# One overlapping 5 KB run per partition for the four shifted k rows, with the front of the convolution done in place

## The chip, the cores and the metric

The kernel runs on one core of one Trainium2 chip. The metric is device time in microseconds (us), the median over executions; a figure called "span" is the length of one profiled execution, about 2 us shorter than its time. Inside an execution, times count from the start of the span.

## The reference, cut to what matters

```python
def _A_ref(q, k, v, shift_k, ssm_k, ssm_D):          # B, S, D = 1, 2048, 640; ks = 4
    k_pad = jnp.pad(k, ((0, 0), (ks - 1, 0), (0, 0)))
    k_shift = jnp.zeros_like(k)
    for t in range(ks):
        k_shift = k_shift + k_pad[:, t:t + S, :] * shift_k[:, ks - 1 - t][None, None, :]
    kv = k_shift * v
    # ... long convolution of kv with ssm_k by FFT, plus kv * ssm_D, gives y
    return q * y
x = A_q
h = x + _A_ref(_layernorm(x), A_k, A_v, A_shift_k, A_ssm_k, A_ssm_D)
h2 = h + _B_ref(_layernorm(h), B_w_gate, B_w_up, B_w_down)   # silu(x@gate) * (x@up) @ down
```

Each output row needs four neighbouring rows of k. The kernel cuts the 2,048 rows into four blocks of 512 and each block into two halves of 256 rows.

## The kernel before

For each half of a block, the "front" loads four shifted copies of k (k0 to k3, 0.33 MB each) and v, multiplies and adds them to kv, mirrors the first half through TensorE (kvr), and forms the sum and the difference xe and xo (the tile xeo). TensorE then transforms xeo to X. VectorE multiplies X with the transformed filter G and accumulates into A; TensorE transforms A back ("inverse"); after a layer norm the rows hl are transposed by DMA into hT, and the up and down products of the FFN follow.

```python
def conv_front(j, p_load, p_calc):
    kv = []
    for half in (0, 1):
        ...                                             # block 0 uses other tiles and queues
            ks = [front.tile([P, 2, D], BF16, name=f"k{jj}", bufs=2 if jj == 0 else 1) for jj in range(4)]
            v = front.tile([P, 2, D], BF16, name="v")
        for jj in range(4):
            load2(eng, ks[jj][:], kk, j, half, jj)      # four loads, each shifted by one row
        load2(eng, v[:], vv, j, half)
        for jj in range(4):
            nc.vector.tensor_mul(ks[jj][:], ks[jj][:], w4[:, jj:jj + 1, :].to_broadcast([P, 2, D]))
        ...                                             # three adds, times v -> ks[0] is kv
        if half == 0:
            kvr = front.tile([P, 2, D], BF16, name="kvr")
            mirror(ks[0], kvr)
    xeo = front.tile([P, 4, D], BF16, name="xeo")       # own tile for xe and xo
    nc.vector.tensor_add(xeo[:, 0:2, :], kv[1][:], kvr[:])
    nc.vector.tensor_sub(xeo[:, 2:4, :], kv[1][:], kvr[:])
    return xeo
...
prio(1500)                                              # the 2 MB of down weights
wd = big.tile([P, NF, D], BF16, name="wd")
nc.sync.dma_start(out=wd[:, 0:13, :], in_=...)       # and a small load of the rest
...
def inverse(A, x, xln):                                 # twice per block: two hl, two transposes
    ...
        nc.sync.dma_start_transpose(hT[:, :, q * P:(q + 1) * P], hl[:])
```

## Time and profile before

| kernel before | value |
|---|---|
| time, median of three (a fourth, taken later, makes it 316.98) | 316.9 us (316.35 to 317.23) |
| span of the profiled execution | 315.9 us |
| VectorE (DVE) busy in all | 237.6 us (75%) |
| TensorE (PE) busy in all | 277.0 us (88%) |

The first view is busy time by stretch, cut at three events: the first y of block 0 (VectorE at 60.19 us), 100 us, and the end of VectorE's last accumulation (246.64 us). Columns: the stretch, its length, then busy time with instruction count for PE, weight loads, DVE, ACT and POOL, then the granted TensorE clock and the DMA share.

```profile
core 0: us, PE busy (x) PEld busy (x) DVE busy (x) ACT busy (x) POOL busy (x), PEclk, DMA share, GB/s
0.00:60.19 60.19, 35.27 (x227) 22.90 (x228) 39.16 (x54) 29.46 (x51) 9.83 (x18) 1.00 0.79 231
60.19:100.00 39.81, 35.89 (x208) 21.16 (x207) 37.08 (x52) 33.34 (x67) 4.61 (x3) 0.91 0.55 157
100.00:246.64 146.64, 140.78 (x767) 72.70 (x765) 140.24 (x187) 83.23 (x172) 20.11 (x10) 1.00 0.52 138
246.64:315.90 69.26, 65.11 (x382) 35.91 (x382) 21.14 (x44) 22.46 (x46) 5.58 (x6) 0.99 0.30 81
```

Length minus DVE busy is VectorE's idle time: 2.73 us from 60 to 100, and 6.40 us in the 146.64 us after. In both stretches VectorE is nearly full; then 69 us of matmuls remain. So the kernel ends when the last accumulation ends, plus the tail.

The next view is VectorE's timeline near 90 us. `k_1375`, `k_1403`, `k_1373` and `k_1400` are tiles of block 2; xeo at 89.74 is block 1's.

```profile
start us, us, engine line op out<-in xcount [idle before <-releaser]
...
85.30 0.82 DVE L174 TENSOR_TENSOR k_1375<-k_1375,k_1376 128x1280 bf16<-128x1280 bf16 x1
...
89.00 0.82 DVE L172 TENSOR_TENSOR k_1403<-k_1403,w_92 128x1280 bf16<-128x1280 bf16 x1
89.74 0.82 DVE L182 TENSOR_TENSOR xeo<-k_765,kvr 128x1280 bf16<-128x1280 bf16 x1
...
95.36 0.82 DVE L172 TENSOR_TENSOR k_1373<-k_1373,w_92 128x1280 bf16<-128x1280 bf16 x1
96.09 0.82 DVE L172 TENSOR_TENSOR k_1400<-k_1400,w_92 128x1280 bf16<-128x1280 bf16 x1
```

Read: while VectorE would otherwise wait for other engines, it works on the k of the next block. Call this the filler.

SyncE's queue in the same stretch:

```profile
69.95 0.37 SPq L108 DMA_DIRECT2D v<-in_A_v_dram  x1
70.99 2.53 SPq L306 DMA_TRANSPOSE hT<-hl  x2
75.07 0.37 SPq L419 DMA_DIRECT2D wd<-in_B_w_down_dram  x1
77.24 3.81 SPq L306 DMA_TRANSPOSE hT<-hl  x2
```

Last, VectorE at the start, and TensorE at the tail:

```profile
32.48 0.83 DVE L172 TENSOR_TENSOR k_738<-k_738,w_92 128x1280 bf16<-128x1280 bf16 x1 [1.39 <-DMA k_738<-in_A_k_dram]
...
37.87 0.82 DVE L182 TENSOR_TENSOR xeo<-A_103,kvr 128x1280 bf16<-128x1280 bf16 x1
```

```profile
261.79 3.53 PE L346 MATMUL pf<-wd,tT 128*128 128x320 bf16 x24
265.25 1.25 PE L326 MATMUL pf<-hT,wg 128*128 128x512 bf16 x5
266.34 1.24 PE L328 MATMUL pf<-hT,wu 128*128 128x512 bf16 x5
```

At 32.48 the first multiply of block 1's k waited 1.39 us for one quarter of it (`k_738`); xeo of block 0 follows at 37.87.

### The profile page before, as it was taken

To read this page: it belongs to the slowest core of one execution; us is meant where nothing else is said; L and a number is where in the kernel's file an instruction comes from. 1 tells how busy PE (TensorE), PEld (TensorE's weight loads), DVE (VectorE), ACT (ScalarE), POOL (GpSimd) and SP (SyncE) were. 2 spreads that over 40 slices of the span, in tenths; PEclk is the share of its full clock that TensorE was granted. 3 is DMA by queue.
4 is the path that set the end of the run, shared out by engine and by line. 5 is a ranking of instruction groups with operands and counts; after the bars stand their busy time and mean duration, and the time that the engine had idled before them with its cause. 6 is when DMAs were issued, how large, how long until landed. Compare 5 with 4: busy or idle time off the path is not lost.

```text
span 315.9 us, 4310 instructions
## 1 busy us (share of the span) xinstructions
PE 277.0 (88%) x1580; PEld 152.7 (48%) x1580; DVE 237.6 (75%) x334; ACT 168.5 (53%) x334; POOL 40.1 (13%) x37
## 2 busy tenths in 40 slices
PE   1048779699989999997999899989999999999994
PEld 0035447455645454663444456644454665444562
DVE  0069889988999999999989999899969852221111
ACT  0083885289798449302996447059684461455200
POOL 8001010012001001252010003600010040000020
PEclk9999999969999999999999999999999999999999
DMA  7999990227764446915954546435613333553011
GB/s 229 354 330 227 325 266 1 85 84 186 219 180 114 123 126 182 192 46 155 292 153 140 140 121 163 75 118 144 166 42 106 85 82 84 146 151 100 2 42 42
DMA packets 73114, 45.94 MB, mean 145 GB/s; under 512 B 26107, under 2 KB 72245, under 8 KB 73094
## 3 DMA queue, kind: packets, MB, share of 16 engines
q1 hardware_dynamic: 70800, 41.06, 48.0%
q0 software_dynamic: 848, 2.98, 2.7%
q10 hardware_dynamic: 1446, 1.64, 1.7%
q8 instruction: 12, 0.20, 0.3%
q14 instruction: 8, 0.07, 0.1%
HBM read 38.46 MB, written 2.62 MB: 130 GB/s over the span
## 4 chain that ended last, share of the span: by engine, by line
DVE 43%; PE 25%; ACT 10%; DMA 9%; issue 6%; SPq 4%; POOL 2%; ACTq 0%; POOLq 0%; DVEq 0%
PE pf L346 10%; PE pf L326 5%; PE pf L328 5%; DVE tT L335 4%; DVE T L227 4%; PE ps L191 3%; SPq L379 3%; DMA WX<-const_wx 3%; DVE T L220 3%; DVE T L225 3%; DVE o L351 2%; DVE T L218 2%; DMA A_102<-in_A_k_dram 2%; DMA k_741<-in_A_k_dram 2%; DVE A_1421 L221 2%
## 5 line engine op out<-in xcount | busy, mean ns | idle before, releaser
L326 PE MATMUL pf<-hT,wg 128*128 128x512 bf16 (+1 forms) x280 | 71.1, 379 | 2.4 <-DVE o L351 1.9
L328 PE MATMUL pf<-hT,wu 128*128 128x512 bf16 (+1 forms) x280 | 71.9, 379 | 0.0
L346 PE MATMUL pf<-wd,tT 128*128 128x320 bf16 x448 | 64.8, 300 | 0.0
L332 ACT ACTIVATE sg<-pf 128x512 bf16<-128x512 f32 (+1 forms) x56 | 33.2, 594 | 42.1 <-PE pf L328 42.1
L346 PEld LDWEIGHTS <-tT 128*128 128x128 bf16 x448 | 41.1, 97 | 23.6 <-issue 9.0
L335 DVE TENSOR_TENSOR tT<-sg,uc 128x512 bf16<-128x512 bf16 (+1 forms) x56 | 23.4, 419 | 27.0 <-ACT uc L334 26.8
L326 PEld LDWEIGHTS <-wg 128*128 128x128 bf16 (+1 forms) x280 | 27.2, 98 | 32.6 <-issue 3.5
L328 PEld LDWEIGHTS <-wu 128*128 128x128 bf16 (+1 forms) x280 | 27.6, 99 | 30.6
L191 PEld LDWEIGHTS <-tT 128*128 128x128 bf16 x256 | 26.7, 104 | 18.7 <-issue 6.8
L191 PE MATMUL ps<-wd,tT 128*128 128x320 bf16 x192 | 31.7, 329 | 4.1 <-POOL wd L393 1.8
L334 ACT CAST uc<-pf 128x512 bf16<-128x512 f32 (+1 forms) x56 | 32.5, 581 | 0.0
L245 ACT ACTIVATE junk<-x 128x640 bf16<-128x640 bf16 x32 | 23.8, 744 | 5.9 <-DVE x L299 4.8
L356 POOL DMA_INDIRECT out_dram<-o,idx x8 | 15.7, 1964 | 78.9 <-DVE o L351 50.0
L201 PE MATMUL ps<-xeo,WX 128*128 128x320 bf16 x128 | 20.6, 298 | 5.0 <-ACT junk L245 1.5
L351 DVE TENSOR_TENSOR o<-pf,x 128x640 bf16<-128x640 f32 x16 | 13.1, 819 | 15.4 <-PE pf L346 15.3
L246 ACT ACTIVATE junk<-x 128x640 bf16<-128x640 bf16 x32 | 23.9, 748 | 0.5
L121 ACT CAST x<-ps 128x640 bf16<-128x640 f32 x8 | 5.2, 694 | 32.0 <-DVE o L351 32.0
L201 PEld LDWEIGHTS <-WX 128*128 128x128 bf16 x128 | 12.2, 97 | 14.4 <-issue 7.4
L384 PE MATMUL ps<-G_98,ones 1*128 1x320 bf16 x8 | 2.6, 451 | 17.3 <-ACT w_92 L385 13.9
L172 DVE TENSOR_TENSOR A_102<-A_102,w_92 128x1280 bf16<-128x1280 bf16 x4 | 3.1, 819 | 18.6 <-ACT w_92 L385 18.6
L284 ACT COPY es<-ps 128x640 f32<-128x640 f32 x8 | 5.5, 692 | 15.3 <-PE ps L281 15.3
L385 ACT ACT_TABLE_LOAD x1 | 1.3, 1283 | 16.5 <-DMA A_102<-in_A_k_dram 16.5
(223 smaller groups left out, 364.8 us busy)
## 6 DMA issues: line engine op xcount, KB each, us to landing
wg<-in_B_w_gate_dram SPq DMA_DIRECT2D x24, 320.0 KB, 3.3
wu<-in_B_w_up_dram SPq DMA_DIRECT2D x24, 320.0 KB, 3.8
wd<-in_B_w_down_dram SPq DMA_DIRECT2D x1, 2080.0 KB, 8.4
v<-in_A_v_dram SPq DMA_DIRECT2D x6, 320.0 KB, 4.0
A_103<-in_A_k_dram POOLq DMA_DIRECT2D x4, 320.0 KB, 7.8
x<-in_A_q_dram SPq DMA_DIRECT2D x4, 320.0 KB, 5.0
xln<-in_A_q_dram SPq DMA_DIRECT2D x4, 320.0 KB, 3.3
out_dram<-o SPq DMA_DIRECT2D x8, 160.0 KB, 1.8
```

The lines of the kernel that those rows point to most:

```text
L191: nc.tensor.matmul(ps[:, h, 0:NH], WG[:, kt, ct * P:(ct + 1) * P], gT[p][:, kt, h * NH:(h + 1) * NH], start=(kt == 0), stop=(kt == 3))
L201: nc.tensor.matmul(ps[:, h, 0:NH], WX[:, kt, ct * P:(ct + 1) * P], xeo[:, odd + kt, h * NH:(h + 1) * NH], start=(kt == 0), stop=(kt == 1))
L245: nc.scalar.activation(junk[:], src, ACT.Copy, scale=1.0 / D, accum_out=mv[:, 0:1])
L246: nc.scalar.activation(junk[:], src, ACT.Square, scale=D ** -0.5, accum_out=mv[:, 1:2])
L326: nc.tensor.matmul(pg[:z, :], wg[:, kt, cc * P:cc * P + z], hT[:, kt, :], start=(kt == 0), stop=(kt == 4))
L328: nc.tensor.matmul(pu[:z, :], wu[:, kt, cc * P:cc * P + z], hT[:, kt, :], start=(kt == 0), stop=(kt == 4))
L332: nc.scalar.activation(sg[:z, :], pg[:z, :], ACT.Silu)
L334: nc.scalar.copy(uc[:z, :], pu[:z, :])
L335: nc.vector.tensor_mul(tT[:z, c * MB:(c + 1) * MB], sg[:z, :], uc[:z, :])
L346: nc.tensor.matmul(ps[:, h, 0:NH], tT[:z, c * MB + m * P:c * MB + (m + 1) * P], wd[:z, c, h * NH:(h + 1) * NH], start=(c == 0), stop=(c == ...
L351: nc.vector.tensor_add(r3(o[:]), ps[:, :, 0:NH], r3(x[:, m, :]))
L356: nc.gpsimd.indirect_dma_start(out=oo[:, :], out_offset=bass.IndirectOffsetOnAxis(ap=idx[:, 2 * j + m - 2:2 * j + m - 1], axis=0), in_=o[: ...
```

## The change

Its intent: fewer and larger DMAs. A partition's four shifted rows are neighbours in memory, so one run of 5,120 bytes holds them all; one load of 1.31 MB replaces four. kvr, xe and xo then go into the slots of the two k tiles that are no longer needed. The start is cleaned up too: ScalarE issues 5 DMAs in place of 12, two constants share a load, and block 0's v comes in one load.

```diff
-    def load2(eng, dst, t, j, half, shift=0):
+    def load_k(eng, dst, j, half):
+        def rows(r0, n, m):
+            return bass.AP(kk.tensor, kk.offset + r0 * D, [[D, n], [P * D, m], [1, 4 * D]])
+        dst = dst.rearrange("p m s d -> p m (s d)")
+        r0 = j * MB + 256 * half - 3
         if r0 >= 0:
+            eng.dma_start(out=dst, in_=rows(r0, P, 2))
+            return
+        ...                                   # first rows of the sequence
@@ conv_front
-                ks = [front.tile([P, 2, D], BF16, name=f"k{jj}", bufs=2 if jj == 0 else 1) for jj in range(4)]
+                t = front.tile([P, 2, 4, D], BF16, name="k", bufs=2)
+                load_k(nc.sync, t[:], j, half)
...
+            for s in (3, 2, 1, 0):
+                nc.vector.tensor_mul(ks[s], ks[s], w4[:, 3 - s:4 - s, :].to_broadcast([P, 2, D]))
...
-                kvr = front.tile([P, 2, D], BF16, name="kvr")
-                mirror(ks[0], kvr)
-        xeo = front.tile([P, 4, D], BF16, name="xeo")
+                mirror(ks[3], ks[2])
+        (_, _, kvr, _), (_, xe, xo, kv) = halves
+        nc.vector.tensor_add(xe, kv, kvr)
+        nc.vector.tensor_sub(xo, kv, kvr)
```

More of the change, by code (lines that the diff above doesn't have):

```diff
@@ L98, with load2 @@
     idx = cpool.tile([P, 2 * NB], mybir.dt.int32, name="idx")
-    I_h = nc.inline_tensor(np.eye(P, dtype=np.float32).astype(ml_dtypes.bfloat16), name="const_i")
-    ident = cpool.tile([P, P], BF16, name="ident")
-    J_h = nc.inline_tensor(np.eye(P, dtype=np.float32)[::-1].astype(ml_dtypes.bfloat16), name="const_j")
-    J = cpool.tile([P, P], BF16, name="J")
-    def load2(eng, dst, t, j, half, shift=0):
-        r0 = j * MB + 256 * half - shift
-        if r0 >= 0:
-            eng.dma_start(out=dst, in_=t[r0:r0 + 256, :].rearrange("(m p) d -> p m d", p=P))
-        else:
-            nc.gpsimd.memset(dst[0:shift, 0, :], 0.0)
-            eng.dma_start(out=dst[shift:16, 0, :], in_=t[0:16 - shift, :])
-            eng.dma_start(out=dst[16:P, 0, :], in_=t[16 - shift:P - shift, :])
-            eng.dma_start(out=dst[:, 1, :], in_=t[P - shift:2 * P - shift, :])
+    IJ_h = nc.inline_tensor(np.concatenate([np.eye(P), np.eye(P)[::-1]], axis=1).astype(ml_dtypes.bfloat16),
+                            name="const_ij")
+    IJ = cpool.tile([P, 2 * P], BF16, name="IJ")
+    ident, J = IJ[:, 0:P], IJ[:, P:2 * P]
+    def load2(eng, dst, t, j, half):
+        r0 = j * MB + 256 * half
+        eng.dma_start(out=dst, in_=t[r0:r0 + 256, :].rearrange("(m p) d -> p m d", p=P))
+    def load_k(eng, dst, j, half):
[3 more added lines that the diff above has]
+        r0 = j * MB + 256 * half - 3
+        if r0 >= 0:
+            eng.dma_start(out=dst, in_=rows(r0, P, 2))
+            return
+        eng.dma_start(out=dst[16:P, 0:1, :], in_=rows(13, 112, 1))
+        eng.dma_start(out=dst[:, 1:2, :], in_=rows(P - 3, P, 1))
+        eng.dma_start(out=dst[3:16, 0:1, :], in_=rows(0, 13, 1))
+        nc.gpsimd.memset(dst[0:3, 0:1, :], 0.0)
+        for p in range(3):
+            nc.gpsimd.dma_start(out=dst[p:p + 1, 0, (3 - p) * D:4 * D],
+                                in_=bass.AP(kk.tensor, kk.offset, [[D, 1], [1, (p + 1) * D]]))
     def mirror(src, dst):
@@ L119, in mirror @@
             for h in range(2):
-                nc.tensor.matmul(ps[:, h, 0:NH], J[:], src[:, 1 - m, h * NH:(h + 1) * NH], start=True, stop=True)
+                nc.tensor.matmul(ps[:, h, 0:NH], J, src[:, 1 - m, h * NH:(h + 1) * NH], start=True, stop=True)
             nc.scalar.copy(r3(dst[:, m, :]), ps[:, :, 0:NH])
@@ L149 @@
     k0a, k0b, v0 = sp("A0"), sp("A1"), G[3]
-    wrow = G[2][0:1, 0:4, :].rearrange("p a b -> p (a b)").rearrange("p (d j) -> p d j", j=4)
+    wflat = G[2][0:1, 0:4, :].rearrange("p a b -> p (a b)")
+    wrow = wflat.rearrange("p (d j) -> p d j", j=4)
     ones = cpool.tile([1, P], BF16, name="ones")
@@ L154, in conv_front @@
     def conv_front(j, p_load, p_calc):
-        kv = []
+        halves = []
         for half in (0, 1):
@@ L158, in conv_front @@
             if j == 0:
-                eng = nc.gpsimd if half else nc.scalar
-                t = k0b if half else k0a
-                ks = [t[:, 2 * jj:2 * jj + 2, :] for jj in range(4)]
+                t = (k0b if half else k0a)[:].rearrange("p (m s) d -> p m s d", s=4)
+                load_k(nc.gpsimd if half else nc.scalar, t, j, half)
                 v = v0[:, 2 * half:2 * half + 2, :]
-            else:
-                eng = nc.sync
-                ks = [front.tile([P, 2, D], BF16, name=f"k{jj}", bufs=2 if jj == 0 else 1) for jj in range(4)]
+                if half == 0:
+                    nc.scalar.dma_start(out=v0[:, 0:4, :], in_=vv[0:MB, :].rearrange("(m p) d -> p m d", p=P))
+            else:
+                t = front.tile([P, 2, 4, D], BF16, name="k", bufs=2)
+                load_k(nc.sync, t[:], j, half)
@@ L166, in conv_front @@
                 v = front.tile([P, 2, D], BF16, name="v")
-            for jj in range(4):
-                load2(eng, ks[jj][:], kk, j, half, jj)
-            load2(eng, v[:], vv, j, half)
+                load2(nc.sync, v[:], vv, j, half)
+            ks = [t[:, :, s, :] for s in range(4)]
             prio(p_calc + 50 * half)
-            for jj in range(4):
-                nc.vector.tensor_mul(ks[jj][:], ks[jj][:], w4[:, jj:jj + 1, :].to_broadcast([P, 2, D]))
-            nc.vector.tensor_add(ks[0][:], ks[0][:], ks[1][:])
@@ L174, in conv_front @@
-            nc.vector.tensor_add(ks[2][:], ks[2][:], ks[3][:])
-            nc.vector.tensor_add(ks[0][:], ks[0][:], ks[2][:])
-            nc.vector.tensor_mul(ks[0][:], ks[0][:], v[:])
-            kv.append(ks[0])
-            if half == 0:
-                kvr = front.tile([P, 2, D], BF16, name="kvr")
-                mirror(ks[0], kvr)
-        xeo = front.tile([P, 4, D], BF16, name="xeo")
-        nc.vector.tensor_add(xeo[:, 0:2, :], kv[1][:], kvr[:])
-        nc.vector.tensor_sub(xeo[:, 2:4, :], kv[1][:], kvr[:])
@@ L184, in conv_front @@
-        return xeo
+            for s in (3, 2, 1, 0):
+                nc.vector.tensor_mul(ks[s], ks[s], w4[:, 3 - s:4 - s, :].to_broadcast([P, 2, D]))
+            nc.vector.tensor_add(ks[3], ks[3], ks[2])
+            nc.vector.tensor_add(ks[1], ks[1], ks[0])
+            nc.vector.tensor_add(ks[3], ks[3], ks[1])
+            nc.vector.tensor_mul(ks[3], ks[3], v[:])
+            if half == 0:
+                mirror(ks[3], ks[2])
+            halves.append(ks)
+        (_, _, kvr, _), (_, xe, xo, kv) = halves
@@ L186, in g_transform @@
+        nc.vector.tensor_add(xe, kv, kvr)
+        nc.vector.tensor_sub(xo, kv, kvr)
+        return xe, xo
     def g_transform(p):
@@ L196, in x_transform @@
         for ct in (0, 1, 4, 5, 2, 3, 6, 7):
-            odd = 2 if ct in (2, 3, 4, 5) else 0
+            src = xeo[1] if ct in (2, 3, 4, 5) else xeo[0]
             ps = psA.tile([P, 2, 512], FP32, name="ps")
@@ L201, in x_transform @@
                     nc.tensor.matmul(ps[:, h, 0:NH], WX[:, kt, ct * P:(ct + 1) * P],
-                                     xeo[:, odd + kt, h * NH:(h + 1) * NH], start=(kt == 0), stop=(kt == 1))
+                                     src[:, kt, h * NH:(h + 1) * NH], start=(kt == 0), stop=(kt == 1))
             nc.scalar.copy(r3(X[j][:, ct, :]), ps[:, :, 0:NH])
@@ L365 @@
     prio(0)
-    nc.scalar.dma_start(out=wrow, in_=bass.AP(A_shift_k.tensor, A_shift_k.offset, [[4 * D, 1], [4, D], [1, 4]]))
+    nc.scalar.dma_start(out=wflat, in_=bass.AP(A_shift_k.tensor, A_shift_k.offset, [[4 * D, 1], [1, 4 * D]]))
     nc.sync.dma_start(out=g0raw, in_=A_ssm_k[:, 0:MB].rearrange("(c p) l -> p c l", p=P))
-    nc.gpsimd.dma_start(out=ident[:], in_=I_h.ap())
+    nc.gpsimd.dma_start(out=IJ[:], in_=IJ_h.ap())
     nc.gpsimd.dma_start(out=Drow[:], in_=A_ssm_D.partition_broadcast(1))
@@ L372 @@
     prio(90)
-    nc.sync.dma_start(out=J[:], in_=J_h.ap())
     nc.sync.dma_start(out=WX[:], in_=WX_h.ap())
@@ L390 @@
             for c in range(5):
-                nc.tensor.transpose(ps[:, s, c * P:(c + 1) * P], g0raw[:, c, l0:l0 + P], ident[:])
+                nc.tensor.transpose(ps[:, s, c * P:(c + 1) * P], g0raw[:, c, l0:l0 + P], ident)
         nc.vector.tensor_copy(gT[0][:, 2 * t:2 * t + 2, :], ps[:, :, 0:D])
```

## The prediction

> **What bounds the kernel now.** Times from the span's start (315.9 us, profiled). Busy time by stretch: from 98 to 247 us VectorE works 142.5 of 149 us, TensorE 143.1; from 62 to 98 ScalarE 31.4 of 36; from 247 on only TensorE, 64.8 of 69. The chain of waits follows VectorE until the last accumulation of block 3 ends (246.7), then 69 us of matmuls: the end is "that accumulation" plus 69 us. Before 37 us DMA bounds the start (about 350 GB/s, engines full), and ScalarE, which issues 12 DMAs in order and starts work at 16.5 us.
>
> **What the change does.** Bytes stay: each k row is still read four times, in runs of 5,120 bytes, not 1,280. VectorE's work stays: ten 1,280-element operations for each half, 0.74 us apart. ScalarE issues 5 DMAs instead of 12, SyncE 17 fewer. kvr and xeo move into k slots.
>
> *Packets.* 1,280-byte packets took 55 ns (median), 5,120-byte ones 227: the same per byte. But the Trainium skill ("DMA: Bandwidth & Descriptors", Queues, rings and completion order) says that an engine goes round its queues by packet. The trace agrees: from 9 to 15 us GpSimd's queue (5,120-byte packets) took 69% of engine time, SyncE's (1,024) 21%. Now ScalarE's k loads have 5,120-byte packets too, beside SyncE's g0raw, WG, WX and x.
>
> *Start.* ScalarE is free 9 us earlier, but third in its order is the statistic of x, behind 2.2 MB on SyncE's queue. About 5.8 MB must move first; estimate x at 19 us (before 17.2). It gates w4's second half, the transposes and the copies into gT (22.2 us before). Estimate: -1 to +1 us.
>
> *k of block 1.* Before, the first of four loads landed at 32.4 us; VectorE waited 1.4 us and multiplied while the others came. Now one 1.31 MB load must land whole: about 35 us (estimate: 30.4 when the transposing loads end, 3.6 for the bytes at 365 GB/s, 1 to land). The instruction order puts a multiply by it before the last two operations of block 0's front. The wait grows to 3.5-4.5 us and xeo of block 0 comes near 41 us instead of 37.9: +2.5 to +3 us.
>
> *Lost filler.* From 62 to 98 us, where ScalarE limits, VectorE did eight operations on k of block 2 (5.9 us). Now xe, xo and kvr sit in the two k buffers, so block 2's load waits for block 1's x_transform; only 1.5 us of xln work moves forward. So 4.4 us of VectorE work moves into the bound stretch, whose 6.5 us of VectorE idleness absorbs perhaps half: +2 us.
>
> Sum about +4 us; as I may overrate the wait, 320 us.
>
> **Predicted: 319.5 us, 8 in 10 between 314 and 324.5.** Faster by over 2%: 0.04; within: 0.83; slower: 0.13.
>
> **What would show it.** ScalarE's first instruction near 7-9 us, then a wait of some 8 us for x; k of block 1 landing near 35 us, VectorE waiting over 3 us for it; the first x_transform matmul near 42 us (38.8 before); no k work of block 2 on VectorE before 95 us; VectorE's total within 2 us of 237.6; the tail still 69 us.
>
> **What would make it wrong.** x landing well before 18 us (the start gains 2-3 us); the k load landing by 33 us; VectorE's idleness absorbing all; in-place operations slower than 0.74 us; TensorE waiting for the last hT, as only 62 matmuls now follow the last inverse (101 before).

## More of the kernel before

SyncE issues nearly all DMAs, in one order fixed at build time: k, v, the transposes of hl, wd and the weights share it. And each engine's order is chosen at build time from the priorities (`prio`) and a simulated readiness, so an edit in one place can reorder instructions in another.

At 265 us the up products of block 3 follow the down products of block 2 without a gap, five matmuls in 1.09 us (266.34 - 265.25).

## The result, and the profile after

| | before | after |
|---|---|---|
| time, median | 316.98 us (316.35 to 317.23) | 331.67 us (329.64 to 333.56) |
| ratio | 1 | 1.0465, 95% interval 1.0388 to 1.0542 |

A ratio here is the mean time of one kernel's fast runs over that of the other's of the same rounds, so it is not quite the ratio of the medians. The change is slower by 14.7 us; the prediction said 2.6 us, with an upper bound of 324.5. The profiled execution is the slowest of four (span 331.5), so differences in this profile are somewhat larger than the median's.

Busy time by stretch, cut at the same events (62.57, 100, 261.22 us):

```profile
core 0: us, PE busy (x) PEld busy (x) DVE busy (x) ACT busy (x) POOL busy (x), PEclk, DMA share, GB/s
0.00:62.57 62.57, 36.88 (x220) 23.34 (x221) 39.27 (x54) 29.33 (x51) 8.98 (x15) 0.97 0.71 219
62.57:100.00 37.43, 29.77 (x178) 17.54 (x178) 28.56 (x39) 28.02 (x57) 3.09 (x2) 0.95 0.45 112
100.00:261.22 161.22, 153.60 (x840) 79.96 (x838) 150.46 (x202) 89.92 (x183) 20.01 (x12) 0.99 0.51 142
261.22:331.50 70.28, 62.30 (x343) 32.90 (x343) 19.84 (x42) 22.35 (x45) 5.41 (x6) 0.95 0.27 73
```

The 15.6 us between the two spans add up: +2.38 us until the first y (62.57 - 60.19), +12.20 us from there to the last accumulation, +1.02 us of tail. Of the 12.20 us, 1.70 is more VectorE work and 10.50 is VectorE idle time: 8.87 us now against 2.73 before 100 us, and 10.76 against 6.40 after it. VectorE has no more to do; it waits.

VectorE near 97 us, where all k named is block 1's until 107.40, when the first work on block 2's k begins:

```profile
90.11 1.49 DVE L227 TENSOR_TENSOR G_937<-X_285,G_97 128x2560 bf16<-128x2560 bf16 x1
97.08 0.42 DVE L346 TENSOR_TENSOR tT<-sg,uc 128x512 bf16<-128x512 bf16 x1 [5.47 <-ACT uc L345]
97.42 0.82 DVE L193 TENSOR_TENSOR k<-k 128x1280 bf16<-128x1280 bf16 x1
98.15 0.82 DVE L194 TENSOR_TENSOR k<-k 128x1280 bf16<-128x1280 bf16 x1
...
107.40 0.81 DVE L184 TENSOR_TENSOR k<-k,w_91 128x1280 bf16<-128x1280 bf16 x1
```

The filler is gone. Lines 193 and 194 form xe and xo from kv and kvr. kvr lies in the first half's k tile, which can be loaded again only when xo has been formed; xe and xo lie in the second half's, which must wait until TensorE has read them. SyncE's queue shows it, and the first wait of TensorE:

```profile
75.24 0.53 SPq L107 DMA_DIRECT2D v<-in_A_v_dram  x1
76.78 0.37 SPq L429 DMA_DIRECT2D wd<-in_B_w_down_dram  x1
79.08 4.94 SPq L317 DMA_TRANSPOSE hT<-hl  x2
...
99.03 6.29 SPq L116 DMA_DIRECT2D k<-in_A_k_dram  x2
```

```profile
89.69 1.44 PE L337 MATMUL pf<-hT,wg 128*128 128x512 bf16 x3 [3.11 <-DMA hT<-hl]
```

The first k load of block 2 is issued at 99.03 us, when xo has just been formed (98.15 + 0.82). The second pair of hT is issued at 79.08 us behind wd and lands 10.6 us later (89.69 - 79.08), where TensorE has waited 3.11 us.

The start, first ScalarE's wait for x and then VectorE's for k:

```profile
20.46 0.74 ACT L256 ACTIVATE junk<-x 128x640 bf16<-128x640 bf16 x1 [9.23 <-DMA x<-in_A_q_dram]
```

```profile
34.80 0.82 DVE L184 TENSOR_TENSOR k<-k,w_91 128x1280 bf16<-128x1280 bf16 x1 [2.57 <-DMA k<-in_A_k_dram]
...
40.70 0.81 DVE L193 TENSOR_TENSOR A_102<-A_102,A_101 128x1280 bf16<-128x1280 bf16 x1
```

TensorE at the tail:

```profile
265.36 9.11 PE L357 MATMUL pf<-wd,tT 128*128 128x320 bf16 x62
278.54 2.31 PE L337 MATMUL pf<-hT,wg 128*128 128x512 bf16 x5 [4.08 <-DMA hT<-hl]
280.65 2.34 PE L339 MATMUL pf<-hT,wu 128*128 128x512 bf16 x5
282.78 1.73 PE L337 MATMUL pf<-hT,wg 128*128 128x512 bf16 x5
284.35 1.24 PE L339 MATMUL pf<-hT,wu 128*128 128x512 bf16 x5
```

TensorE waits 4.08 us for the last hT. Then the first 15 up products take 5.81 us (284.35 - 278.54), where 15 at the pace of the kernel before (1.09 us for five) would take 3.3. That fits the Trainium skill, "TensorE: Matmul & The Clock Gate", § What's actually happening: after an idle window of about 3.4 us TensorE runs at half clock until it has been busy for such a window. This trace agrees: the granted clock is 0.50 in every 2 us slice from 278 to 282 us and 1.00 from 284. In the whole tail it is 0.95, against 0.99 before.

### The profile page after: what moved, and what is told of

Same layout as the page of the kernel before. It is cut to its first block, busy times and chain, and to the rows that moved or that the text cites. A ratio compares the mean times of both kernels' runs of the same rounds, so it can differ in the third digit from the quotient of the medians.

```text
span 331.5 us, 4265 instructions
## 1 busy us (share of the span) xinstructions
PE 282.5 (85%) x1580; PEld 153.7 (46%) x1580; DVE 238.1 (72%) x334; ACT 169.6 (51%) x334; POOL 37.5 (11%) x34
## 4 chain that ended last, share of the span: by engine, by line
DVE 42%; PE 23%; issue 12%; DMA 8%; ACT 7%; POOL 6%; SPq 1%; POOLq 0%; ACTq 0%; DVEq 0%
PE pf L337 6%; PE pf L339 6%; DMA x<-in_A_q_dram 5%; PE pf L357 5%; PE ps L202 3%; DVE tT L346 3%; DMA hT<-hl 3%; DVE T L231 3%; DVE T L236 3%; DVE T L229 3%; DVE k L184 2%; DVE T L238 2%; ACT junk L256 2%; DVE o L362 2%; DVE hl L268 2%
## 5 line engine op out<-in xcount | busy, mean ns | idle before, releaser
L337 PE MATMUL pf<-hT,wg 128*128 128x512 bf16 (+1 forms) x280 | 73.9, 392 | 10.9 <-DMA hT<-hl 7.2
L339 PE MATMUL pf<-hT,wu 128*128 128x512 bf16 (+1 forms) x280 | 73.2, 388 | 0.0
L357 PEld LDWEIGHTS <-tT 128*128 128x128 bf16 x448 | 41.2, 97 | 24.2 <-issue 8.8
L202 PEld LDWEIGHTS <-tT 128*128 128x128 bf16 x256 | 25.9, 102 | 18.1 <-issue 5.0
L202 PE MATMUL ps<-wd,tT 128*128 128x320 bf16 x192 | 30.4, 317 | 4.4 <-DVE y L308 1.8
L256 ACT ACTIVATE junk<-x 128x640 bf16<-128x640 bf16 x32 | 23.8, 743 | 17.3 <-DMA x<-in_A_q_dram 9.2
L367 POOL DMA_INDIRECT out_dram<-o,idx x8 | 14.3, 1793 | 106.9 <-DVE o L362 74.4
L184 DVE TENSOR_TENSOR k<-k,w_91 128x1280 bf16<-128x1280 bf16 x24 | 19.3, 815 | 2.6 <-DMA k<-in_A_k_dram 2.6
L212 PE MATMUL ps<-k,WX 128*128 128x320 bf16 x96 | 15.5, 298 | 1.4 <-DVE k L193 1.3
L401 PE MATMUL ps<-IJ,SP 128*128 128x128 bf16 x20 | 2.3, 312 | 9.9 <-ACT w_91 L395 9.9
```

The lines of the kernel that those rows point to most:

```text
L184: nc.vector.tensor_mul(ks[s], ks[s], w4[:, 3 - s:4 - s, :].to_broadcast([P, 2, D]))
L202: nc.tensor.matmul(ps[:, h, 0:NH], WG[:, kt, ct * P:(ct + 1) * P], gT[p][:, kt, h * NH:(h + 1) * NH], start=(kt == 0), stop=(kt == 3))
L212: nc.tensor.matmul(ps[:, h, 0:NH], WX[:, kt, ct * P:(ct + 1) * P], src[:, kt, h * NH:(h + 1) * NH], start=(kt == 0), stop=(kt == 1))
L256: nc.scalar.activation(junk[:], src, ACT.Copy, scale=1.0 / D, accum_out=mv[:, 0:1])
L337: nc.tensor.matmul(pg[:z, :], wg[:, kt, cc * P:cc * P + z], hT[:, kt, :], start=(kt == 0), stop=(kt == 4))
L339: nc.tensor.matmul(pu[:z, :], wu[:, kt, cc * P:cc * P + z], hT[:, kt, :], start=(kt == 0), stop=(kt == 4))
```

## The experiments

All ratios are over the kernel before, run on the same chip. All outputs are right. Kernels named a_ start from the change, those named b_ from the kernel before with a part of the change, those named before_ from the kernel before without any of it. One slip in the recorded texts: where they speak of a first product or a sum "of block 1" at 36 to 44 us, it is block 0's. At 90 us and later it is block 1's. Only before_vlate has 1 inside its interval.

| run | time, us | ratio (95% interval) |
|---|---|---|
| the change | 331.67 | 1.0465 (1.0388 to 1.0542) |
| b_start: new start only | 323.37 | 1.0218 (1.0183 to 1.0252) |
| b_blocks: new blocks 1 to 3 only | 327.67 | 1.0327 (1.0282 to 1.0372) |
| a_out: kv, kvr, xeo out of the k tile | 325.95 | 1.0292 (1.0261 to 1.0323) |
| a_split_1: block 1's k in four loads | 334.47 | 1.0556 (1.0512 to 1.0600) |
| a_split_1r: the same, in reading order | 331.17 | 1.0437 (1.0389 to 1.0484) |
| a_wdpool: wd through GpSimd | 342.36 | 1.0792 (1.0735 to 1.0849) |
| b_start_wdpool | 332.47 | 1.0519 (1.0488 to 1.0550) |
| b_start_xlate: x later | 328.31 | 1.0352 (1.0292 to 1.0413) |
| a_wdlate: wd after the transposes | 330.21 | 1.0407 (1.0380 to 1.0435) |
| before_wdlate: the same, control | 324.90 | 1.0255 (1.0229 to 1.0281) |
| b_start_xfirst: x earlier | 321.62 | 1.0145 (1.0125 to 1.0164) |
| b_start_wdx: both | 323.51 | 1.0201 (1.0179 to 1.0222) |
| before_holdk: filler removed | 323.51 | 1.0206 (1.0155 to 1.0256) |
| before_vlate: v after hT | 318.27 | 1.0053 (0.9991 to 1.0115) |
| b_sxf_front: earlier mirror | 324.61 | 1.0250 (1.0200 to 1.0300) |
| a_warm3: TensorE kept busy | 331.84 | 1.0441 (1.0386 to 1.0496) |

### Splitting the change: b_start and b_blocks

```diff
# b_start: the change's start and block 0; blocks 1 to 3 keep four loads, four tiles, kvr and xeo
+                kt = [front.tile([P, 2, D], BF16, name=f"k{jj}", bufs=2 if jj == 0 else 1) for jj in range(4)]
# b_blocks: the kernel before's start; blocks 1 to 3 as in the change
+            t = front.tile([P, 2, 4, D], BF16, name="k", bufs=2)
```

> The kernel before with only the new start (block 0's k as 5 KB runs, merged constants, 5 DMAs on ScalarE); blocks 1 to 3 load k as before into their own tiles. My theory (the loss is made in blocks 1 to 3): 316 to 320 us, xeo of block 0 within 1.5 us of 37.9. Rival (the start, where large packets crowd out SyncE's loads, is the cause): 325 us or more.

> The kernel before with its own start; only blocks 1 to 3 load k as one run and are done in place in two tiles. My theory: 327 to 333 us, nearly all of the loss; no operation on k of block 2 on VectorE before block 1's first product. Rival (the start): 316 to 319 us. Rival (only the two together lose): under 323 us.

Measured: +6.9 us for the start (0.0218 of 316.8), between my theory and its rival, and +10.4 us for the blocks, as expected. Their sum, 17.3, is above the 14.7 of the whole, but within the intervals; in the profiled executions the parts add up, as the spans grow by 4.8 us (320.7 - 315.9) and 10.6 us (326.5 - 315.9), and by 15.6 in the change. The loss is not all in the in-place blocks, as the prediction's sum had it; the start, costed there at -1 to +1 us, loses on its own. In b_start the first y of block 0 comes at 60.57 us, only 0.4 later than before; but TensorE waits 2.94 us for hT at 87.19, and the stretch from the first y to the last accumulation is 4.8 us longer. In b_blocks the first y comes at 62.34 us, 2.2 later than before, and that stretch is 7.9 us longer, though TensorE does not wait for hT of block 0. The first up products of block 0, in b_start and then in b_blocks:

```profile
87.19 1.13 PE L341 MATMUL pf<-hT,wg 128*128 128x512 bf16 x3 [2.94 <-DMA hT<-hl]
```

```profile
86.52 0.81 PE L350 MATMUL pf<-hT,wg 128*128 128x512 bf16 x3
```

### Taking the held buffers away: a_out

```diff
-                t = front.tile([P, 2, 4, D], BF16, name="k", bufs=2)
+                t = front.tile([P, 2, 4, D], BF16, name="k")
-            nc.vector.tensor_add(ks[3], ks[3], ks[1])
-            nc.vector.tensor_mul(ks[3], ks[3], v[:])
+            kv = front.tile([P, 2, D], BF16, name="kv", bufs=2)
+            nc.vector.tensor_add(kv[:], ks[3], ks[1])
+            nc.vector.tensor_mul(kv[:], kv[:], v[:])
```

(kvr, xe and xo also get one tile of their own. A third k buffer, the plainer test, was not run; I found that it did not fit the on-chip memory, which no run on record shows.)

> The changed kernel with the one-run loads kept, but kv, kvr and xeo in tiles of their own again (k in one buffer, kv in two), so block 2's first k load no longer waits for block 1's transform; the order then has eight operations on block 2's k before block 1's first product, as before. Theory that the held buffers are the larger part: 321 to 326 us, xeo of block 0 still near 40.7. Rival (the shape of the load is what costs): 329 us or more.

Measured: 325.95 us, 5.7 us less than the change. From the first y to the last accumulation it takes 189.57 us, not 198.65 (before: 186.45), and VectorE does four multiplies of the next k between 82.9 and 89.4 us. The first y comes 2.2 us later; 1.5 us of that is there at block 0's first product (43.13 us against 41.61), which needs xe, and this edit forms xe after xo. So the held buffers cost the change several us, by a test that also changes the tiles and the order.

### The wait for the whole run: a_split_1 and a_split_1r

```diff
 def load_k(eng, dst, j, half):
+    if j == 1:
+        for s in (3, 2, 1, 0):       # a_split_1: ascending; a_split_1r: in the order of the multiplies
+            eng.dma_start(out=dst[:, :, s * D:(s + 1) * D], in_=kk[r0 + s:r0 + s + 256, :]...)
+        return
```

> The changed kernel, in place, but block 1's two k tiles loaded slot by slot in four DMAs; blocks 2 and 3 still by one run. VectorE's order is unchanged. Theory: VectorE's wait of 2.6 us before block 1's first multiply falls to about 1 us or less, xeo of block 0 comes 1.5 to 3 us sooner (38 to 39), total 328 to 330 us (1.5 to 3 us less than the change). Rival (the wait is absorbed later): within 1 us of the change, 331 to 332.

> The change with the k tiles of block 1 alone filled by four slot loads again, this time in the order in which VectorE reads the slots (slot 3 first), so that the first multiply needs a quarter of the tile. It mends the flaw of a_split_1, which loaded slot 3 last. If the wait for the whole 1.31 MB run is what makes the first product of block 1 late, VectorE's 2.57 us wait shrinks below 1 us, the sum xe is ready at 38 to 39.5 us instead of 40.7, the first product of block 1 starts at 39 to 40.5 us instead of 41.6, and the time is 328.5 to 330.5 us. Rival: what the four loads carry is the same number of bytes with smaller packets (1,280 B), so the last slot and v land later and the sum is no earlier than 40.5 us; then the time stays at 331 to 334 us, as a_split_1 did (334.5).

a_split_1 was a badly made test: it loaded last the slot that VectorE reads first, and the wait was 3.34 us. In a_split_1r the wait is gone, xe of block 0 comes at 38.00 us and the first product at 38.9, as in the kernel before. That half of the expectation was met; the time, 331.17 us, was not below 330.5. In the profile the first y comes at 59.89 us, 2.7 earlier than in the change. VectorE then idles longer up to 100 us, 10.62 us (40.11 - 29.49), but less after it (9.07), in all 19.7 as in the change, and the stretch to the last accumulation is as long (198.90 us against 198.65). The span is 1.8 us shorter, so the gain at the start was not plainly lost. The four-run times cannot tell 331.2 from 331.7.

### The hT transposes and wd: a_wdpool, b_start_wdpool, a_wdlate, before_vlate

```diff
# a_wdpool, b_start_wdpool
-    nc.sync.dma_start(out=wd[:, 0:13, :], ...)
+    nc.gpsimd.dma_start(out=wd[:, 0:13, :], ...)
# a_wdlate: wd must wait for block 0's last hl
+    nc.gpsimd.tensor_copy(wd[0:1, 0, 0:1], last_hl[0][0:1, 0:1])
     nc.sync.dma_start(out=wd[:, 0:13, :], ...)
# before_vlate: v of block 2 must wait for block 0's first hl
+                nc.gpsimd.tensor_copy(v[0:1, 0, 0:1], hls[0][0:1, 0:1])
```

> The change with the loads of wd (2 MB) issued by GpSimd instead of SyncE, nothing else. Theory: the 3.11 us that TensorE waits for hT of block 0 at 89.7 us come from SyncE's order, in which the second pair of hT transposes stands behind wd. Then the wait falls below 0.7 us, up of block 0 starts at 86.5 to 87.5 us, and the first product of block 1 comes 2 to 3 us earlier than 98.3; the time is 327 to 330 us if the gain carries to the end. Rival: VectorE's work for block 1 is the chain and absorbs it, and the time stays within 1 us of 331.7.

> The kernel before with the new start (b_start, 323.4 us) and wd loaded through GpSimd. If SyncE's order at 70 to 82 us is what b_start loses, up of block 0 starts at 84 to 85 us instead of 87.2, TensorE does not wait for hT (2.94 us in b_start), and the time is 317 to 320 us. Rival: the loss of b_start is in the extra time at the start and in VectorE's order, and the time stays at 322 to 324 us.

> The change, with the big load of wd held back on SyncE's own queue until block 0's last hl exists (GpSimd copies one element of that hl into wd, and the load must wait for it), so that the second pair of hT transposes is issued ahead of it. It mends what a_wdpool had wrong: there wd ran beside the transposes instead of ahead of them, and TensorE waited 12.3 us. Theory (the 3.11 us wait is the queue order): the wait for hT falls below 0.7 us, up of block 0 starts at 86 to 87 us instead of 89.7, and the time is 327 to 330 us if VectorE's 5.5 us wait at 97 us shrinks with it. Rival: the wait goes elsewhere (the down products wait for wd, or VectorE stays short of work), and the time stays at 331 to 334 us.

> The kernel before, with the v load of block 2 held until block 0's first hl exists, so that SyncE issues it after the first pair of hT transposes and just ahead of wd, as in the change. The order of TensorE, VectorE and ScalarE is exactly that of before. If this order is what makes the second hT pair late, TensorE waits 2 to 3.5 us for hT of block 0 and its up starts at 87 to 88 us instead of 84.9; the time rises to 318.5 to 321 us. Rival: the order of one 0.33 MB load does nothing, up starts at 85 us and the time stays at 316 to 318 us; then the late hT of the change comes from its later start.

a_wdpool was far off: 342.4 us. The transposes, issued at 79.49 us, landed 13.8 us later:

```profile
93.32 0.59 PE L337 MATMUL pf<-hT,wg 128*128 128x512 bf16 x1 [12.27 <-DMA hT<-hl]
```

b_start_wdpool lost in the same way (332.5). The Trainium skill, "DMA: Bandwidth & Descriptors", § Rules for kernel authors, says that spreading DMAs over issuing engines gives no bandwidth, as all use the same DMA engines. These two runs agree: beside wd, on another queue, the transposes were slower than behind it (13.8 us against 10.6).

a_wdlate puts the transposes ahead of wd. Then they land within 4.0 us (issued at 79.48, first up product at 83.52):

```profile
83.52 0.38 PE L340 MATMUL pf<-hT,wg 128*128 128x512 bf16 x1 [2.48 <-DMA hT<-hl]
```

So the order on the queue does set when hT lands, but the time fell only to 330.2, the ratio by 0.006 (1.8 us), within the intervals: VectorE now waited 3.35 and 2.67 us for ScalarE's copies of G. A wait was removed and another took its place. before_vlate tests my idea that the place of v on SyncE's queue is to blame, with the order of the three compute engines all but unchanged (in the traces VectorE does two instructions at another place). It fell: the wait for hT was 0.6 us, up started at 84.67, the ratio is 1.0053 with 1 inside its interval. In this kernel the pair landed 7.4 us after its issue (84.67 - 77.26), and in the kernel before within 7.7 (84.91 - 77.24, without a wait); why it takes 10.6 us in the change stays open. The traces narrow it: from issue to the first product it is 10.2 to 11.2 us in the change, a_split_1, a_split_1r, a_warm3, b_start, b_start_xfirst and b_start_xlate, all with the new start and three of them with the old blocks, and at most 7.7 in before, before_vlate, before_holdk and b_blocks, all with the old start. So the new blocks are not the cause. The new start alone does not decide it either: b_sxf_front has it and 7.7 us, a_out 8.7.

### How fragile the order is: before_wdlate

```diff
+    nc.gpsimd.tensor_copy(wd[0:1, 0, 0:1], last_hl[0][0:1, 0:1])
     nc.sync.dma_start(out=wd[:, 0:13, :], ...)
```

> Control: the kernel before with the same hold on wd, where TensorE waited for no hT. The edit moves nothing that was on the critical path, but it reorders the instructions of all engines a little (the compiler's static schedule follows every edit). If such reordering alone costs several us, as a rival for the whole loss of the change has it, the time is 320 us or more; if it costs little, the time is 315 to 319 us.

This control, expected at 315 to 319 us if reordering costs little, came out at +8.1 us. But it is not neutral: it copies one element, and by that holds back a 2 MB load. One cause is in view. wd now stands ahead of the first k load of block 2 that was still missing, and VectorE, in order, waits for it:

```profile
95.29 0.82 DVE L172 TENSOR_TENSOR k<-k,w 128x1280 bf16<-128x1280 bf16 x1 [6.00 <-DMA k<-in_A_k_dram]
```

So 60 to 100 us is a stretch in which v, four transposes, 2 MB of wd and the next k share one queue, and the kernel before does best in its own order. An edit there can cost several us, whatever it is meant to do; it need not, as before_vlate, which holds back v by a copy of the same kind, cost nothing clear. What reordering alone costs, no run shows.

### The start: b_start_xlate, b_start_xfirst, b_start_wdx, b_sxf_front

```diff
# b_start_xlate: load_x(0) at priority 140, not 110      # b_start_xfirst: WX at 120, not 90, behind x
-    prio(110)                                            -    prio(90)
+    prio(140)                                            +    prio(120)
     xin[0], xln[0] = load_x(0, nc.sync)                       nc.sync.dma_start(out=WX[:], in_=WX_h.ap())
# b_start_wdx: b_start_xfirst and the hold on wd         # b_sxf_front: b_start_xfirst and conv_front(0, 10, 40), not 200
```

> b_start with the load of x of block 0 given a lower priority, so that ScalarE's four copies of the convolution weights come before the statistics of x and TensorE's first transposes need not wait for x (ScalarE waited 9.23 us for x in the changed kernel and all of it stood ahead of the weight copies). If the wait for x is what holds the start, the first G product begins at 18 to 20 us instead of 25.7 and VectorE's first multiply of k comes some us earlier; the first product of block 1 then starts at 36 to 39 us instead of 39.4 and the time is 319 to 322 us. Rival: the k of block 1 lands no earlier than before, so block 1's first product stays within 0.7 us of 39.4 and the time stays at 322 to 325 us.

> b_start with SyncE's loads of x (0.66 MB) ahead of the load of WX (0.52 MB); nothing else moves on TensorE, VectorE or ScalarE. ScalarE waited 9.2 us for x in b_start, and the second pair of weight copies and TensorE's first transposes stood behind that wait. Expected: x is there 2 to 4 us earlier than 20.5, the first G product starts at 22 to 24 us instead of 25.7, the first product of block 1 at 36 to 38 us instead of 39.4; the time falls from 323.4 to 319 to 322 us. Rival: WX or the k of block 1 is then the late one, and the time stays at 323 to 325 us.

> b_start with both: x ahead of WX and wd held behind block 0's transposes. A candidate to beat the kernel before (316.3 us on the last chip). If b_start loses through the late x and the late hT, both go and the time is 313 to 317 us; up of block 0 starts at 82 to 84 us and no wait for hT is over 1 us. If the rest of its loss lies in VectorE's order, it stays at 318 to 322 us.

> b_start_xfirst (321.6 us) with a higher priority for the arithmetic of block 0's front, so that TensorE mirrors kv of block 0 between the first G products instead of after all 64 of them (VectorE's xeo of block 0 stood behind that mirror). A candidate to beat the kernel before. If the mirror gates the start, xeo of block 0 comes 1 to 2 us earlier than 38.3 and the time is 318 to 321 us; if the queue on SyncE at 70 to 85 us decides, the time follows the wait for hT there instead (2.75 us in b_start_xfirst).

b_start_xlate moved the first G product to 21.25 us, but x was now issued behind the long transposes on SyncE (26.96), and ScalarE waited 20 us for it in front of the G copies; the first product of block 0 slipped to 44.2. b_start_xfirst moved only loads: the first G product came 1.3 us earlier (24.47), block 0's first product stayed at 39.2, the time fell by 2.3 us by the ratios. It is the best of the versions with the new start, still 4.6 us slower than before. b_start_wdx and b_sxf_front, each meant to beat the kernel before, did not; the second delayed G and brought the first y to 64.05 us. No version tried beat the kernel before.

### The filler alone: before_holdk

```diff
+            if j == 2 and half == 0:
+                for jj in range(4):
+                    nc.gpsimd.tensor_copy(ks[jj][0:1, 0, 0:1], xeo[1][0:1, 2, 0:1])
             for jj in range(4):
                 load2(eng, ks[jj][:], kk, j, half, jj)
```

> The kernel before, with the four k loads of block 2's first half held until xo of block 1 has been made (GpSimd copies one element of xo into each tile), which is when the change's buffer comes free. Nothing else of the change is in it. The prediction costed this lost filler at 2 us, because the idle time of VectorE in the bound stretch would absorb half of 4.4 us; undoing it in the change (a_out) gave 5.7 us. If the filler is the large part, the time is 321 to 326 us, VectorE does no k work of block 2 before block 1's first product, and its idle time from 60 to 100 us rises from 2.7 to 6 to 9 us. If the prediction's sum was right for this term, the time is 318 to 320 us.

Measured: 323.51 us, +6.5 us, inside the range. Nothing of the change is in this kernel but the moment at which the k of block 2's first half may be loaded. Its stretches (cut at its first y, 100 us and last accumulation), and its first work on block 2's k:

```profile
60.03:100.00 39.97, 35.63 (x218) 20.83 (x216) 34.46 (x50) 34.16 (x69) 6.05 (x7) 1.00 0.52 149
100.00:253.20 153.20, 142.84 (x789) 74.42 (x787) 143.92 (x191) 83.14 (x170) 18.09 (x10) 1.00 0.51 138
```

```profile
96.39 1.55 DVE L175 TENSOR_TENSOR k<-k,w 128x1280 bf16<-128x1280 bf16 x2
```

VectorE idles 5.51 us up to 100 us (before: 2.73; I had expected at least 6) and 9.28 us after (before: 6.40). TensorE waits for no hT of block 0 here; in the tail it waits 2.86 us for the last one (at 270.52), much as in the change. The prediction had 4.4 us of work moving into the later stretch and half of it absorbed by idle time there. After 100 us VectorE has 3.7 us more work (143.92 - 140.24), so the amount was about right; but nothing was absorbed, as idle time grew by 2.9 us as well. A caution: like before_wdlate, this edit reorders other instructions too, so the 6.5 us are those of the held load and the order that the build made around it, as in the change.

### The half clock after a wait: a_warm3

```diff
+    def keep_warm(p, pool_, name, n):                     # 16 products that nobody reads
+        prio(p)
+        ps = pool_.tile([P, 2, 512], FP32, name=name)
+        for i in range(n):
+            nc.tensor.matmul(ps[:, 0, :], WI[:, 0, 0:P], last_hl[0][:, 0:512], start=True, stop=True)
...
+        if j == 3:
+            keep_warm(40000, psA, "ps", 16)
         tT[j] = ffn_up(j, hT[j], z + 5000, z - 1000)
```

> The change plus 16 matmuls of 512 columns on TensorE just before the up products of block 3, into a PSUM tile that nobody reads (they take the last hl and WI, so they start when the transposes of hT do). No other engine's order changes by one instruction. In the change TensorE waited 4.08 us there for hT, the granted clock then stood at 0.5 for two windows of 3.41 us, and the first 15 up products took 5.8 us where 15 later ones take 3.2. If the clock after a wait is a cost of its own, the wait is filled (16 times 0.216 is 3.5 us), the half clock window at the tail vanishes, the first 15 up products take 3.2 to 4 us, the tail after the last accumulation ends falls from 70.3 to 67.5 to 68.5 us and the time by 1.5 to 3 us, to 328.5 to 330 us. Rival: the dummy products only delay the up products or the clock follows something else; the time is 331 to 333 us.

In the profile all that was expected of the tail came:

```profile
265.93 9.11 PE L366 MATMUL pf<-wd,tT 128*128 128x320 bf16 x62
275.56 3.63 PE L292 MATMUL ps<-hl,WI 128*128 128x512 bf16 x15 [0.52 <-DVE hl L268]
279.12 1.25 PE L346 MATMUL pf<-hT,wg 128*128 128x512 bf16 x5
280.21 1.24 PE L348 MATMUL pf<-hT,wu 128*128 128x512 bf16 x5
```

The up products run at full pace at once, and the tail from the last accumulation (261.8 us) to the end of the span (329.5) is 67.7 us, not 70.3. The time did not follow clearly: the six executions spread from 328.14 to 332.38, the ratio fell by 0.0024 (0.8 us), far within the intervals, and the median lies in the rival's range of 331 to 333. So the half clock after the wait is shown, at 2.6 us in one profiled execution; a gain in time is not.

## Why the prediction was wrong, point by point

- **"Lost filler", "perhaps half: +2 us".** This is the first of two steps that failed. The mechanism was named rightly: no work on block 2's k before 95 us, because its buffers were held. The size was not. Alone in the kernel before the held load costs 6.5 us (before_holdk), undoing it in the change brings 5.7 us (a_out), and with the new blocks alone (b_blocks) the stretch from the first y to the last accumulation is 7.9 us longer. I had counted VectorE's 6.5 us of idleness in the bound stretch as room to put work into. It is made of short waits for other engines, and it did not shrink: 6.40 us before, 9.28 in before_holdk, 10.76 in the change. So the amount moved was about right (3.7 us in before_holdk, 4.4 predicted), and the absorption was the error. Idle time left over in an almost full engine was not free time.
- **Start, "-1 to +1 us".** This is the second step that failed, and by its size at least as large an error. The local events were right: ScalarE's first instruction at 8.65 us (7 to 9 predicted), then a wait for x of 9.23 us (8 predicted), x at 20.4 (19 predicted), the copies into gT 1.1 us later (at most 1 predicted). But the start alone (b_start) costs 6.9 us (4.8 in the profiled span), nearly all of it after the first y of block 0, where the prediction did not look. b_start_xfirst returns 2.3 us of that. The remaining 4.6 us show as 4.9 us more idle time of VectorE from the first y on, in waits of at most 2.1 us, and as a wait of 2.75 us of TensorE for hT. I did not find one cause. That before_wdlate lost 8.1 us in the same stretch makes the order of that stretch a possible one, but that edit held back wd as well, and before_vlate, which moved only v, lost nothing clear: it is argued, not shown.
- **"k of block 1 ... +2.5 to +3 us".** Right as an event: the load landed for a multiply at 34.80 us (35 predicted), xeo of block 0 came at 40.70 (41 predicted), 2.83 us later, though the wait was 2.57 us and not over 3. Not settled as a term of the sum: with the wait removed (a_split_1r) the start was back at its old times and the span was 1.8 us shorter, but by the ratios the total fell by 0.9 us, and the intervals allow nothing as well as the 2.5 to 3 us predicted.
- **Arbitration by packet.** I used it to place x; x came 1.4 us later than the estimate. No run tested the packet size alone.
- **"The tail still 69 us."** It was 70.3 us, and the danger I had listed ("TensorE waiting for the last hT") came true: 4.08 us, followed by a half clock that I had not listed. b_blocks, with the same blocks and the old start, has the same wait (4.1 us). The tail grew by only 1.0 us because 39 of its matmuls (382 - 343) had moved ahead of it, so that TensorE was busy 2.8 us less there (65.11 - 62.30) in spite of the half clock.
- **Right without qualification.** VectorE's total (238.1 us, 0.5 us above before): in-place operations are not slower. The direction, although only 0.13 had been put on slower by over 2%. The bound: the end still follows the last accumulation.
- **What stays open.** How the loss of the start comes about. What else than the filler is in the 10.4 us of b_blocks: its first y is 2.2 us later, and its tail 0.6 us longer. Why the second pair of hT lands after 10.6 us, and not within 7.7 as before, is not settled. Nor is the spread of 4 us between executions of the change.

## What to carry to other kernels

Before putting results into a load's buffer to save space, ask when that buffer can be loaded again, and what the engine that bounds the kernel does meanwhile; the double buffer here was double in name only. The Trainium skill, "Trainium Kernel Development and Optimization", § Best Practices, asks for double buffering so that DMA overlaps compute: in this change one buffer was held until block 1's xo was formed and the other until xe and xo were read, and the next load was issued at 99.03 us, with VectorE's work on it starting at 107.40 where before it had begun at 78.89. And in a kernel tuned to one static order, measure control edits before giving a few us to a mechanism, and make sure that they are neutral: of the two here that copy one element to hold back a load, the one on wd cost 8.1 us and the one on v nothing clear.

## What the Trainium skill lacked or had wrong

- "DMA: Bandwidth & Descriptors", § Rules for kernel authors, advises coalescing many small transfers into one large one. That rule names no price beside it, though elsewhere the skill allows that splitting a DMA may let work start sooner. Here four loads of 0.33 MB let the first multiply start at 32.48 us, the single one of 1.31 MB at 34.80.
- The same page gives rates for DMA transposes, but not what a big load does to a small transposing one. Here a pair of transposes landed 4.0 us after its issue ahead of a 2 MB load, 7.4 us (before_vlate) to 11.2 us (a_warm3) behind it on the same queue, and 13.8 us beside it on another queue.
- "TensorE: Matmul & The Clock Gate", § What's actually happening, ties the half clock to an idle window of about 3.4 us. At 89.69 us in the change a wait of 3.11 us, near that length, was followed by slow products too (three in 1.44 us, where three at full pace take 0.81 in the kernel before). The profile of before shows a granted clock of 0.50 from 62 to 68 us (0.91 between 60 and 100) although the longest wait of TensorE listed from 56 us to there was 1.25 us, while before_holdk has 1.00 in the whole stretch. So shorter waits were enough in one execution.
- No page of it warns that, in a program whose engine orders are fixed at build time, a one-element copy that holds back one load can move the whole by 2.6% (before_wdlate, 1.0255) or by nothing clear (before_vlate, 1.0053).
